# Eleven constant full-array matmuls a chunk between the reordering matmuls of a decode-attention kernel

## The chip, the cores and the metric

One core of one Trainium2 chip. The metric is the device time of one execution, in microseconds (us); times quoted are medians of the fast runs, three to eleven per kernel. A ratio compares runs of two kernels in the same rounds, and is not quite the ratio of the medians that are quoted beside it. One profiled run of each kernel gives the views shown.

## The reference, cut to what matters

Two attention decode steps with one query position each, concatenated. A has 32 query heads on 8 key heads and a window of 2048 keys; B has 32 heads, batch 4 and 8192 keys each.

```python
def _B_ref(x, k_cache, v_cache, wq, wo):
    B, Sq, D = x.shape                      # 4, 1, 512
    H, Dh = 32, 128
    q = (x @ wq).reshape(B, Sq, H, Dh) ...  # transposed to (B, H, Sq, Dh)
    scores = jnp.einsum("bhqd,bhkd->bhqk", q, k_cache) * (Dh ** -0.5)
    p = _softmax(scores, axis=-1)
    o = jnp.einsum("bhqk,bhkd->bhqd", p, v_cache)
    return ... @ wo                         # heads joined
```

B's two caches are 537 MB in bf16 (2 x 4 x 32 x 8192 x 128 x 2 bytes), so loading them is most of what the kernel must do.

## The kernel before

B is 32 chunks of 4 heads and one batch entry. A chunk has 256 key tiles and 256 value tiles of 128 x 128. TensorE, VectorE (DVE), ScalarE (ACT) and GpSimd (POOL) are the engines. This is the order in which a chunk's work is given to them; each engine then runs its own list and waits on semaphores (shortened, with comments added):

```python
def whole_B(c):
    ...
    for g in range(ch["NG"]):               # 32 groups of 8 key tiles
        emit_T(ch["s"] + g)                 # TensorE: 8 transposes; DVE or ACT: copy to SBUF
        ...
        if g >= SLAG:
            emit_S(ch["s"] + g - SLAG)      # TensorE: 8 score matmuls
    ...
    stats_rowmax(c, 1)
    reorder(c, 0, 0)                        # TensorE: 4 matmuls, 32 rows x 512 columns each
    reorder(c, 1, 1)
    reorder(c, 2, 2)
    stats_gmax(c)                           # TensorE: transpose of the row maxima; DVE: maximum
    stats_bc(c)                             # TensorE: broadcast; DVE: scaled bias
    exp_B(c)                                # ACT: 8 exponentials
    for u in range(3):
        take_wol(c, u, u)                   # DVE: copy of a reordered block
    reorder(c, 3, 0)                        # waits for take_wol(c, 0)
    take_wol(c, 3, 0)
    sums_B(c)
    for g in range(ch["NG"]):
        emit_pv(c, g)                       # TensorE: 8 value matmuls into the bank "po"
    ...
    norm_out(c)
```

`reorder(c, u, bank)` brings the output weights of the chunk's four heads into the order that the last product needs; block `u` uses the array rows 32u to 32u+31. `emit_pv` waits for the first four exponentials and for the values. The next chunk's values are loaded when the product of this chunk is done; its keys when the transposes of this chunk are. In the views `tr` takes transposes and reordered weights, `sc` scores, `ms` the small statistics, `po` the value product and `fin` the last product; `kv` holds keys or values, `pbb` the exponentials.

## Time and profile before

| | before |
|---|---|
| time, three runs ahead of the prediction | 1376.5 us |
| span of the profiled run | 1373.0 us |
| TensorE busy, DMA queue busy | 90%, 99.5% |
| mean granted TensorE clock | 0.915 |
| moved by DMA | 587 MB, mean 428 GB/s |

The granted clock is the share of full speed that TensorE was given. The prediction quotes the lines on the bound. What it says of the clock is seen in windows of 1 us in the middle of the span (columns: stretch, its length, busy us of TensorE, weight loads, DVE, ACT and POOL, granted clock, DMA share, GB/s):

```profile
619.00:620.00 1.00, 0.72 (x4) 0.10 (x2) 1.00 (x3) 0.97 (x3) 0.00 (x0) 1.00 0.60 262
620.00:621.00 1.00, 0.00 (x0) 0.00 (x0) 0.45 (x1) 0.96 (x3) 0.00 (x0) 0.65 0.99 426
...
624.00:625.00 1.00, 1.00 (x23) 1.00 (x21) 0.00 (x0) 0.00 (x0) 0.00 (x0) 0.50 1.06 459
...
628.00:629.00 1.00, 1.00 (x40) 1.00 (x37) 0.00 (x0) 0.00 (x0) 0.00 (x0) 1.00 1.07 459
```

The clock is halved at the end of the statistics (1.00 to 0.50 in these windows), and the value product's first microseconds run with it: 23 matmuls are seen in a microsecond, against 40 after the clock is back.

The statistics of the last chunk, in the timeline of TensorE (start, length, engine, line, operation, and in brackets the idle time before it and what ended it):

```profile
1354.86 1.06 PE L421 MATMUL tr<-wos,back 32*128 32x512 bf16 x12
1355.91 0.27 PE L419 MATMUL ms<-identf,rm 128*4 128x128 f32 x1
1356.55 0.38 PE L421 MATMUL ms<-gm,ind 4*128 4x4 f32 x2 [0.37 <-DVE gm L570]
1357.79 1.88 PE L421 MATMUL tr<-wos,back 32*128 32x512 bf16 x4 [0.86 <-DVE kv L716]
1359.60 7.23 PE L421 MATMUL po<-pbb,kv 128*128 128x64 bf16 x168
```

R stands for the start of the first line from here on, as in the prediction: 1354.86 in this chunk. The clock fell at 1357.58, 2.7 us after R, in the gap of 0.86 us, the longest of this timeline; in the 3.42 us up to there TensorE was busy for 2.09 us.

The trace also gives the pace of a reordering matmul of 512 columns: on one row group they start 0.216 us apart with the full clock (618.92, 619.13 and 619.35 in the chunk in the middle) and 0.427 us apart with the half (1358.18, 1358.61 and 1359.04).

### The profile page before, as it was taken

What the parts mean: (1) busy time and instruction counts of PE and PEld (TensorE: products, weight loads), DVE (VectorE), ACT (ScalarE), POOL (GpSimd) and SP (SyncE); (2) the same over time, 40 slices, a digit from 0 to 9 for tenths busy, and PEclk for the clock granted to TensorE, in tenths of its full rate; (3) what the DMA queues carried; (4) which work ended last, traced back from release to release, by engine and by line L of the source; (5) the groups of instructions that cost most, each with busy time, mean ns of one, the idle gap of its engine ahead of it and who ended that gap; (6) DMA issues with size and microseconds to landing.
All of it is one profiled execution on the core that took longest, in us unless ns stands there. A gap on an engine that the chain in (4) does not pass through costs nothing.

```text
span 1373.0 us, 60822 instructions
## 1 busy us (share of the span) xinstructions
PE 1229.9 (90%) x27417; PEld 1134.6 (83%) x27417; DVE 744.4 (54%) x1335; ACT 513.3 (37%) x649; POOL 9.8 (1%) x29
## 2 busy tenths in 40 slices
PE   4897899999898889998889898998988899988998
PEld 4786788889888788898888888987888889887887
DVE  1775456655555556555555565554555555554555
ACT  1553244433333334433333344243333443333333
POOL 2000000000000000000000000000000000000000
PEclk9998899999999999999999999998999899999999
DMA  9999999999999999999999999999999999999997
GB/s 401 425 427 443 422 422 435 432 431 436 437 432 428 431 432 432 434 438 435 433 432 420 433 435 430 437 439 430 428 430 432 431 435 439 433 428 430 422 428 319
DMA packets 21084, 587.52 MB, mean 428 GB/s; under 512 B 2356, under 2 KB 2376, under 8 KB 4808
## 3 DMA queue, kind: packets, MB, share of 16 engines
q1 hardware_dynamic: 21032, 587.21, 99.5%
q8 instruction: 15, 0.25, 0.1%
q14 instruction: 5, 0.04, 0.0%
q10 hardware_dynamic: 32, 0.01, 0.0%
HBM read 587.21 MB, written 0.01 MB: 428 GB/s over the span
## 4 chain that ended last, share of the span: by engine, by line
DMA 52%; PE 43%; DVE 2%; ACT 1%; issue 1%; SPq 0%; POOLq 0%; ACTq 0%; DVEq 0%
DMA kv<-in_B_v_cache_dram 47%; PE po L421 22%; PE tr L419 12%; PE sc L421 6%; DMA kv<-in_B_k_cache_dram 2%; DMA kv<-in_B_wq_dram 2%; PE ms L421 1%; PE tr L421 1%; ACT pbb L601 1%; DMA kv<-in_A_k_cache_dram 1%; PE fin L421 1%; DVE sA L539 1%; DVE kt L486 1%; PE ms L419 0%; DVE gm L570 0%
## 5 line engine op out<-in xcount | busy, mean ns | idle before, releaser
L419 PE MATMUL tr<-identb,kv 128*128 128x128 bf16 x8704 | 663.8, 220 | 9.3 <-POOLq L72 4.2
L484 ACT ACTIVATE kt<-tr 128x1024 bf16<-128x1024 bf16 x352 | 359.3, 1023 | 718.3 <-PE tr L419 718.0
L486 DVE COPY kt<-tr 128x1024 bf16<-128x1024 bf16 x736 | 501.8, 691 | 217.2 <-PE tr L419 214.4
L419 PEld LDWEIGHTS tr<-identb,kv 128*128 128x128 bf16 x8704 | 506.7, 98 | 20.3 <-issue 9.9
L421 PE MATMUL sc<-qq,kt 128*128 128x64 bf16 x8192 | 397.7, 191 | 13.7 <-DVE kt L486 9.8
L421 PEld LDWEIGHTS po<-pbb,kv 128*128 128x128 bf16 x8192 | 305.7, 108 | 74.0 <-issue 43.5
L421 PE MATMUL po<-pbb,kv 128*128 128x64 bf16 x8192 | 309.3, 208 | 51.7 <-POOLq L72 44.8
L421 PEld LDWEIGHTS sc<-qq,kt 128*128 128x128 bf16 x8192 | 331.2, 98 | 17.2 <-DVE kt L486 13.1
L601 ACT ACTIVATE pbb<-sc,negb 32x128 bf16<-32x128 f32 x256 | 137.2, 536 | 121.4 <-DVE negb L584 118.2
L421 PE MATMUL tr<-wos,back 32*128 32x512 bf16 x512 | 81.3, 409 | 27.4 <-DVE kv L716 27.4
L668 DVE RECIPROCAL rinv<-ms 128x4 f32<-128x4 f32 (+1 forms) x40 | 7.8, 196 | 167.5 <-PE ms L421 167.5
L716 DVE CAST kv<-tr 128x512 bf16<-128x512 f32 x128 | 81.2, 684 | 13.1 <-PE tr L421 13.1
L606 DVE TENSOR_REDUCE rsb<-pbb 128x4 f32<-128x1024 bf16 x32 | 39.0, 1220 | 50.9 <-ACT pbb L601 50.9
L421 PEld LDWEIGHTS tr<-wos,back 32*128 32x128 bf16 x512 | 23.5, 97 | 49.7 <-DVE kv L716 30.1
L555 DVE TENSOR_REDUCE rh<-sc 128x4 f32<-128x512 f32 x64 | 43.9, 686 | 14.3 <-PE sc L421 14.3
L690 DVE TENSOR_TENSOR oz<-po,rz 128x16 bf16<-128x16 f32 x32 | 5.6, 175 | 67.3 <-PE po L421 67.3
L421 PE MATMUL sc<-qb,kt 128*128 128x64 bf16 (+3 forms) x512 | 26.1, 196 | 0.6 <-DVE gx L576 0.6
L421 PEld LDWEIGHTS ms<-gm,ind 4*128 4x128 f32 x64 | 9.4, 182 | 18.0 <-DVE gm L570 18.0
L421 PEld LDWEIGHTS sc<-qb,kt 128*128 128x128 bf16 x512 | 21.8, 101 | 1.9 <-DVE gx L576 1.1
L421 PE MATMUL ms<-gm,ind 4*128 4x4 f32 x64 | 12.2, 258 | 11.9 <-DVE gm L570 11.9
L421 PE MATMUL po<-pba,kv 128*128 128x64 bf16 x512 | 20.5, 199 | 2.6 <-ACT pba L623 1.4
L421 PEld LDWEIGHTS po<-pba,kv 128*128 128x128 bf16 x512 | 17.9, 102 | 5.1 <-ACT pba L623 4.2
(63 smaller groups left out, 209.8 us busy)
## 6 DMA issues: line engine op xcount, KB each, us to landing
kv<-in_B_k_cache_dram SPq DMA_DIRECT2D x60, 4096.0 KB, 27.1
kv<-in_A_k_cache_dram SPq DMA_DIRECT2D x8, 2048.0 KB, 13.6
kv<-in_A_v_cache_dram SPq DMA_DIRECT2D x8, 2048.0 KB, 15.2
kv<-in_B_k_cache_dram SPq DMA_DIRECT2D x7, 2048.0 KB, 28.4
kv<-in_B_v_cache_dram SPq DMA_DIRECT2D x3, 4096.0 KB, 21.6
kv<-in_B_v_cache_dram SPq DMA_DIRECT2D x3, 2048.0 KB, 26.1
kv<-in_B_v_cache_dram SPq DMA_DIRECT2D x5, 1024.0 KB, 28.3
kv<-in_A_wq_dram SPq DMA_DIRECT2D x1, 4096.0 KB, 12.4
```

The source lines that it names most:

```text
L419: sch.add("pe", lambda e: e.transpose(o, l, r), waits, key)
L421: sch.add("pe", lambda e: e.matmul(o, l, r, start=start, stop=stop), waits, key)
L484: sch.add("act", lambda e: e.activation(dst, src, ACTF.Copy), waits=waits, key=("ev", s))
L486: sch.add("dve", lambda e: e.tensor_copy(dst, src), waits=waits, key=("ev", s))
L539: emit = lambda e, src=src, b=b: e.scalar_tensor_tensor(out=t, in0=src, scalar=mk[:, b:b + 1], in1=t, op0=ALU.mult, op1=ALU.add)
L555: sch.add("dve", lambda e: e.tensor_reduce(out=rh[:, half, :], in_=src, axis=AX.X, op=ALU.max), waits=[("S", ch["s"] + (half + 1) * ch["NG ...
L601: sch.add("act", lambda e, src=src, dst=dst, pp=pp, u=u: e.activation(dst, src, ACTF.Exp, bias=negb[pp, 0, u:u + 1], scale=scale), waits=[ ...
L606: sch.add("dve", lambda e: e.tensor_reduce(out=rst[1][:, :], in_=probs_of(c).rearrange("p j u -> p u j"), axis=AX.X, op=ALU.add), waits=[( ...
L668: sch.add("dve", lambda e: e.reciprocal(out=ri, in_=ms[:, L0:L0 + n]), waits=[("L", c)], key=("rinv", c))
L690: sch.add("dve", lambda e: e.tensor_tensor(out=o, in0=i0, in1=i1, op=ALU.mult), waits=waits, key=("oT", c))
L716: sch.add("dve", lambda e: e.tensor_copy(wol[:, u, :], o), waits=[("reord", c) if u == 3 else ("reord", c, u)] + [("fin", prev(c))], key=( ...
```

## The change

Its intent is to keep TensorE's array in use while the statistics wait for other engines, so that the clock is not halved. The eleven added matmuls, the fillers, multiply two constants and write the bank `po`, which nobody reads at that time; their result is overwritten by the value product.

```diff
+        def keep_busy(n):
+            for _ in range(n):
+                pe_mm(po[:, :], identb[:, :], sel4[:, :, :].rearrange("p r x -> p (r x)"))
+
         def whole_B(c):
...
             reorder(c, 2, 2)
+            keep_busy(2)
             stats_gmax(c)
+            keep_busy(1)
             stats_bc(c)
             exp_B(c)
             for u in range(3):
                 take_wol(c, u, u)
+            keep_busy(3)
             reorder(c, 3, 0)
+            keep_busy(5)
             take_wol(c, 3, 0)
```

## The prediction

> **What bounds the kernel now.** I read the page's summary first, then busy time and DMA rate by stretch, then the chain of waits, then the timeline of one chunk and of the last one.

> The program is decode attention: 8 chunks of A (135 us), then 32 chunks of B. In a B chunk TensorE transposes and scores 256 key tiles, does a short statistics part (maximum, exponentials, the reordering of the output weights), then multiplies 256 value tiles with the probabilities. The diff touches only that middle part.

> ```profile
> PE 1229.9 (90%) x27417; PEld 1134.6 (83%) x27417; DVE 744.4 (54%) x1335; ACT 513.3 (37%) x649; POOL 9.8 (1%) x29
> ...
> q1 hardware_dynamic: 21032, 587.21, 99.5%
> ...
> DMA 52%; PE 43%; DVE 2%; ACT 1%; issue 1%; SPq 0%; POOLq 0%; ACTq 0%; DVEq 0%
> ```

> Both TensorE (90%) and the DMA queue (99.5%) look full. Which one sets the end is told by the rate in each stretch (columns: stretch, its length, busy us of each engine, granted clock, DMA share, GB/s).

> ```profile
> 516.00:1219.00 703.00, 637.74 (x14347) 590.88 (x14345) 382.24 (x648) 261.34 (x324) 0.00 (x0) 0.91 1.00 433
> 1258.00:1295.30 37.30, 34.66 (x798) 32.45 (x799) 21.24 (x36) 14.54 (x18) 0.00 (x0) 0.95 1.00 425
> 1295.30:1332.10 36.80, 34.69 (x801) 32.49 (x801) 21.18 (x36) 14.53 (x18) 0.00 (x0) 0.95 1.01 427
> 1360.00:1365.00 5.00, 5.00 (x107) 5.00 (x105) 1.62 (x2) 1.54 (x3) 0.00 (x0) 0.56 0.87 349
> 1365.00:1373.00 8.00, 5.22 (x161) 4.80 (x157) 0.96 (x4) 0.00 (x0) 0.00 (x0) 1.00 0.02 8
> ```

> The reader is to see that the DMA share is 1.00 at 425 to 433 GB/s until about 1365 us, whoever the chain names, and that only the last 8 us have no transfer. Bytes over rate: one B chunk is 2 x 8.39 MB, at 433 GB/s 38.7 us. TensorE's own period where it waits for no data (the two stretches from 1258.5) is 36.8 us. So in the long middle TensorE waits some 2 us a chunk for values to land, and time saved there only lengthens the wait. The next lines are one such chunk: the statistics, and the wait for values before the first value matmul.

> ```profile
> 615.76 1.06 PE L421 MATMUL tr<-wos,back 32*128 32x512 bf16 x12
> 616.81 0.27 PE L419 MATMUL ms<-identf,rm 128*4 128x128 f32 x1
> 617.45 0.38 PE L421 MATMUL ms<-gm,ind 4*128 4x4 f32 x2 [0.37 <-DVE gm L570]
> 618.69 1.03 PE L421 MATMUL tr<-wos,back 32*128 32x512 bf16 x4 [0.85 <-DVE kv L716]
> 623.23 6.81 PE L421 MATMUL po<-pbb,kv 128*128 128x64 bf16 x168 [3.50 <-POOLq L72]
> 632.86 28.96 DMA kv<-in_B_v_cache_dram
> ```

> The next values are issued when the product of this chunk ends (632.86) and land 28.96 us later. Of that, 8.39 MB at 433 GB/s is 19.4 us; the other 9.6 us the transfer queues behind keys issued before. Issuing it earlier lets it queue longer, not land earlier.

> **The clock.** In this chunk the granted clock falls to half at 620.35 us and returns at 627.1. I located every fall and return in the B chunks in windows of 0.25 us: all lie on one grid of 3.413 us. Cold, value matmuls come every 53 ns (64 columns at half clock: 1 us holds about 19); warm, 88 take 2.71 us, 30.8 ns each. In the last chunk:

> ```profile
> 1357.79 1.88 PE tr L421 x4
> 1359.67 7.17 PE po L421 x168
> 1367.03 2.60 PE po L421 x88
> 1369.98 0.62 PE fin L421 x8
> ```

> The fall is at 1357.58 and the return at 1364.41, so four reordering matmuls take 1.88 us (1.03 us warm) and 4.74 us of the value product run cold: 89 matmuls that would take 2.73 us warm, a loss of 2.0 us. This is what the change is after.

> [...] 0.50 and 1.00 are the levels, and the grid is 3.413 us. The trace adds that the window need not be idle: the fall at 1357.58 closes a window in which TensorE was busy for some 2.1 of 3.41 us. [...]

> **The change part by part.** Nothing is removed, no DMA or wait is added, and the instruction orders of VectorE, ScalarE and the DMA queue are unchanged. TensorE gets 11 matmuls of 512 columns a chunk, which write a bank nobody reads then: 2 before the maximum's transpose, 1 before its broadcast, 3 before and 5 after the last reordering. [...]

> With R the start of the 12 reordering matmuls, in a chunk that waits for no data: the 12 end issuing about R+0.85, two fillers reach R+1.28, and the transpose, at R+1.05 before, starts 0.25 us late. The one filler fits in the 0.37 us gap before the broadcast, the three in the 0.86 us gap before the last reordering. All the rest shifts by 0.25 us: last reordering at R+3.2, 0.85 us warm, five fillers 1.08 us, so the value product starts at R+5.1. Before, it started at R+4.54 to 4.74 in the last three chunks (bounded by the exponentials or by the cold reordering). Cost: 0.4 to 0.55 us a chunk. Gain, if the clock holds: the product takes 256 x 30.8 ns = 7.9 us plus 0.1.

> Does the clock hold? I weighted each matmul by the share of the array's rows that it uses. Before, the window from R-1.36 to R+2.05 (48% so weighted) was not followed by a fall, that from R-1.05 to R+2.36 (40%) was. A fall thus needs somewhat under half. After the change the worst window (R+0.85 to R+4.26) has 0.43+0.21+0.64+0.21+0.21 = 1.70 of 3.41 us, 50%, without the transpose. It is close, but above. I give 65% that the clock holds where TensorE waits for no data. Where it waits for values, idle time follows the fillers and the clock may fall as before; there it costs nothing.

> **The sum.** The last keys before TensorE leads land at 1258.3 in any case. From there: in the 30th and the 31st B chunk the product ran cold for one window, 3.4 us, a loss of 1.4 us (64 tiles at 53 instead of 30.8 ns), less 0.5 = 0.9 us each; the last saves 2.0 - 0.4 = 1.6. That is 3.4 us. But the last value pieces set a floor:

> ```profile
> kv<-in_B_v_cache_dram SPq DMA_DIRECT2D x2, 256.0 KB, 31.6
> ```

> They are issued up to 1334.4 and land about 1366.0, because the queue is full; earlier issue does not help. The last eight tiles then take 0.25 us: product ends at 1366.25 at the earliest, instead of 1369.6. So the gain is capped at 3.3 us: 1376.5 - 3.3 = 1373.2 us if all holds.

> **The rivals.**
> 1. *The whole cold loss comes back:* 32 chunks x 2.0 us = 64 us, 4.6% faster. For it speak TensorE's 90% and the 43% of the chain. Against it: the DMA share of 1.00 and the 9.6 us of queueing[...]. I give this 1%.
> 2. *The clock falls anyway, and the fillers run cold.* From R+3.2 the last chunk's work is 0.85+1.08+7.9 us warm, with half of the 6.35 us up to the return added: product ends at R+16.1 instead of R+14.7, 1.4 us later; over three chunks up to 4 us, 1380 us. The 50% against a threshold between 40 and 48% speaks against it, the rough weighting for it. 15%.
> 3. *It holds in some of the three chunks* (the grid's phase decides), fillers and gains cancel: 1375 to 1376.5 us. 20%.
> 4. *Fillers delay the middle:* 38.3 us of TensorE work even with cold fillers (36.8+1.5) stays below 38.7 us, and 9.6 us of queue hide a late issue. No effect.

> **Range and chances.** 0.65 x 1373.2 + 0.2 x 1375.7 + 0.15 x 1379 is 1374.6; the most likely outcome is near 1373.5. I say 1374.0, with 1372.0 to 1377.8 for 8 in 10 (the three runs before spread by 1 us). A 2% step is 27.5 us, which only the first rival reaches, or a DMA effect that I don't see.

> **What would show it.** Right: DMA share 1.00 and 433 GB/s in the middle as before; TensorE's wait for values longer by about what it saves; last transfer again near 1365 us; granted clock 1.00 through the last three chunks; product of the last chunk ending about 1366 to 1367. Wrong, if the clock falls within R+2.4 to R+5.8 in the last chunks (step "the clock holds"), if the value product starts much later than R+5.1[...], or if the period of the middle moves off 38.8 us (the DMA bound).

## The result, and the profile after

| | before | after |
|---|---|---|
| time, six runs each | 1376.74 us (1375.67 to 1378.51) | 1373.45 us (1372.49 to 1374.21) |
| ratio | | 0.9975, 95% interval 0.9962 to 0.9988 |
| span of the profiled run | 1373.0 us | 1371.8 us |
| mean granted clock | 0.915 | 0.981 |

The page of the changed kernel, the same three lines as in the prediction:

```profile
PE 1249.8 (91%) x27769; PEld 1110.4 (81%) x27769; DVE 744.0 (54%) x1335; ACT 513.8 (37%) x649; POOL 9.8 (1%) x29
...
q1 hardware_dynamic: 21032, 587.21, 99.6%
...
DMA 57%; PE 39%; DVE 2%; issue 1%; ACT 0%; SPq 0%; POOLq 0%; DVEq 0%
```

and its stretches:

```profile
516.00:1219.00 703.00, 650.00 (x14544) 578.06 (x14544) 382.38 (x648) 261.62 (x324) 0.00 (x0) 0.99 1.00 432
...
1355.00:1360.00 5.00, 4.74 (x36) 1.93 (x37) 3.42 (x8) 2.06 (x4) 0.00 (x0) 1.00 0.98 416
1360.00:1365.00 5.00, 5.00 (x156) 4.65 (x155) 1.51 (x2) 2.27 (x5) 0.00 (x0) 1.00 0.93 375
1365.00:1371.80 6.80, 4.03 (x120) 3.61 (x116) 0.95 (x4) 0.00 (x0) 0.00 (x0) 1.00 0.06 21
```

The clock of the middle went from 0.91 to 0.99 and the bytes per second stayed (433, 432). TensorE's records are busier by 12 us of 703 although the product is faster, because the fillers count as busy. The saving shows only in the last stretches, where the clock is 1.00 and the transfers come to their end.

The last chunk's statistics in the changed kernel:

```profile
1355.21 1.06 PE L421 MATMUL tr<-wos,back 32*128 32x512 bf16 x12
...
1356.20 0.61 PE L421 MATMUL po<-sel,identb 128*128 128x512 bf16 x2
...
1356.65 0.27 PE L419 MATMUL ms<-identf,rm 128*4 128x128 f32 x1
...
1357.29 0.38 PE L421 MATMUL ms<-gm,ind 4*128 4x4 f32 x2 [0.16 <-DVE gm L570]
...
1357.60 0.82 PE L421 MATMUL po<-sel,identb 128*128 128x512 bf16 x3
...
1358.53 1.03 PE L421 MATMUL tr<-wos,back 32*128 32x512 bf16 x4
...
1359.49 1.25 PE L421 MATMUL po<-sel,identb 128*128 128x512 bf16 x5
...
1360.58 5.06 PE L421 MATMUL po<-pbb,kv 128*128 128x64 bf16 x168
```

The reader is to see a price and a gain. The price: the transpose starts at R+1.44 instead of R+1.05, and the product at R+5.37 instead of R+4.74. The gain: 168 value tiles take 5.06 us instead of 7.23, and the reordering of four 1.03 instead of 1.88. From R to the end of the span it was 18.14 us (1373.0 - 1354.86) and is 16.59 us (1371.8 - 1355.21), 1.55 us less.

Where did the middle's time go? The waits of TensorE name it. "POOLq L72" is the relay by which POOL passes on that a transfer has landed; the figures are us in total, times, and the longest. Before:

```profile
PE po L421 <- POOLq L72: 44.8, 23, 3.5
...
PE tr L419 <- POOLq L72: 4.2, 8, 0.7
```

After:

```profile
PE tr L419 <- POOLq L72: 42.3, 26, 1.9
PE po L421 <- POOLq L72: 22.6, 23, 2.0
```

Before, the product waited for values. Now fillers occupy part of that wait, the product ends sooner, and the transposes of the next chunk wait for keys instead: 4.2 us became 42.3. Both waits are for the same queue of transfers, which is full (busy for 99.5% of the span before and 99.6% after).

Even near the end keys gate TensorE once. The chain of waits of the changed kernel, from there to the end (start, us, what; the x173 are five fillers and 168 value tiles):

```profile
1306.73 31.11 DMA kv<-in_B_k_cache_dram
1337.94 0.62 PE tr L419 x8
...
1359.56 6.09 PE po L421 x173
1365.84 2.60 PE po L421 x88
1368.79 0.62 PE fin L421 x8
```

One caution about the pair of profiles: in the run profiled after, values land 1.2 us later throughout (the product of the chunk in the middle starts at 624.39 instead of 623.23), though nothing in the diff changes a transfer, and the profiled run before was a fast one (1374.7 us by its own clock). So the spans differ by 1.2 us and the medians by 3.3. Lengths counted from R don't have this offset.

### The profile page after: what moved, and what is told of

The parts are those of the page before. It is cut to its first block, busy times and chain, and to the rows that moved or that the text cites. A ratio compares the mean times of both kernels' runs of the same rounds, so it can differ in the third digit from the quotient of the medians.

```text
span 1371.8 us, 61526 instructions
## 1 busy us (share of the span) xinstructions
PE 1249.8 (91%) x27769; PEld 1110.4 (81%) x27769; DVE 744.0 (54%) x1335; ACT 513.8 (37%) x649; POOL 9.8 (1%) x29
## 3 DMA queue, kind: packets, MB, share of 16 engines
q1 hardware_dynamic: 21032, 587.21, 99.6%
HBM read 587.21 MB, written 0.01 MB: 428 GB/s over the span
## 4 chain that ended last, share of the span: by engine, by line
DMA 57%; PE 39%; DVE 2%; issue 1%; ACT 0%; SPq 0%; POOLq 0%; DVEq 0%
DMA kv<-in_B_k_cache_dram 36%; DMA kv<-in_B_v_cache_dram 18%; PE tr L419 18%; PE po L421 9%; PE sc L421 8%; DMA kv<-in_B_wq_dram 2%; PE fin L421 1%; PE ms L421 1%; PE tr L421 1%; DMA kv<-in_A_k_cache_dram 1%; DVE sA L539 1%; DVE kt L486 0%; DVE kv L716 0%; ACT pba L623 0%; DVE rm L551 0%
## 5 line engine op out<-in xcount | busy, mean ns | idle before, releaser
L419 PE MATMUL tr<-identb,kv 128*128 128x128 bf16 x8704 | 668.6, 221 | 48.2 <-POOLq L72 42.3
L419 PEld LDWEIGHTS tr<-identb,kv 128*128 128x128 bf16 x8704 | 510.3, 99 | 61.1 <-DVE qq L495 41.2
L421 PE MATMUL sc<-qq,kt 128*128 128x64 bf16 x8192 | 399.3, 192 | 13.5 <-DVE kt L486 9.8
L421 PEld LDWEIGHTS sc<-qq,kt 128*128 128x128 bf16 x8192 | 332.9, 98 | 16.9 <-DVE kt L486 13.1
L421 PEld LDWEIGHTS po<-pbb,kv 128*128 128x128 bf16 x8192 | 250.9, 99 | 37.1 <-issue 20.5
L421 PE MATMUL po<-pbb,kv 128*128 128x64 bf16 x8192 | 253.8, 194 | 24.1 <-POOLq L72 22.6
L421 PE MATMUL po<-sel,identb 128*128 128x512 bf16 x352 | 96.9, 384 | 0.0
L716 DVE CAST kv<-tr 128x512 bf16<-128x512 f32 x128 | 80.0, 683 | 0.0
L421 PE MATMUL tr<-wos,back 32*128 32x512 bf16 x512 | 67.8, 383 | 3.2
L421 PEld LDWEIGHTS po<-sel,identb 128*128 128x128 bf16 x352 | 26.6, 98 | 47.6 <-issue 27.8
L421 PEld LDWEIGHTS tr<-wos,back 32*128 32x128 bf16 x512 | 21.5, 93 | 34.0 <-DVE kv L716 18.9
L570 DVE TENSOR_REDUCE gm<-ms 4x4 f32<-4x128 f32 x40 | 11.2, 279 | 28.6 <-PE ms L419 28.6
L421 PE MATMUL sc<-qb,kt 128*128 128x64 bf16 (+3 forms) x512 | 26.3, 197 | 0.4 <-DVE gx L576 0.4
L421 PEld LDWEIGHTS ms<-gm,ind 4*128 4x128 f32 x64 | 9.4, 182 | 17.5 <-DVE gm L570 17.5
L421 PEld LDWEIGHTS sc<-qb,kt 128*128 128x128 bf16 x512 | 22.1, 102 | 1.6 <-issue 0.9
```

What stands on the lines that cost most here:

```text
L419: sch.add("pe", lambda e: e.transpose(o, l, r), waits, key)
L421: sch.add("pe", lambda e: e.matmul(o, l, r, start=start, stop=stop), waits, key)
L570: sch.add("dve", lambda e: e.tensor_reduce(out=gm[0:C, m, 0:U], in_=src, axis=AX.X, op=ALU.max), waits=[("trm", c)], key=("gmax", c))
L716: sch.add("dve", lambda e: e.tensor_copy(wol[:, u, :], o), waits=[("reord", c) if u == 3 else ("reord", c, u)] + [("fin", prev(c))], key=( ...
```

## The experiments

All runs were timed in five rounds. Two theories on where the 3.3 us come from: *tail*, by which the middle is bound by transfers and only TensorE's time in the last three chunks reaches the end; and *middle*, by which each of the 32 chunks gives about 0.1 us. Two on the means: the fillers act by the *activity of the array*, or any instruction on TensorE would do.

### Half of the value product left out

```diff
-            for t in range(TG):
+            for t in (range(TG) if c < NCA else (0, 2, 5, 7)):   # in emit_pv
```

> The changed kernel with half of the value matmuls of B left out (tiles 0, 2, 5 and 7 of each eight; the result is wrong on purpose, all bytes are still loaded): TensorE works about 3.9 us less in every B chunk, 125 us in all. Theory 'transfers bound the middle': only the tail shrinks; last value piece lands about 1366 to 1367 us as before, the end comes at most 2 us sooner, 1371 to 1373 us, ratio 0.996 to 0.9975, 431 to 433 GB/s in the middle. Rival 'TensorE sets part of the middle': 1330 us or lower, over 2% faster.

Measured: 1371.71 us (before in the same rounds 1377.23), ratio 0.9962 (0.9949 to 0.9975); the result is wrong, as meant. Its middle, its wait for keys, and the end of its chain:

```profile
516.00:1219.00 703.00, 609.47 (x12223) 533.76 (x12239) 383.72 (x648) 262.01 (x324) 0.00 (x0) 0.94 1.00 432
```

```profile
PE tr L419 <- POOLq L72: 123.0, 30, 5.6
```

```profile
1330.02 36.23 DMA kv<-in_B_v_cache_dram
1366.99 0.62 PE fin L421 x8
```

TensorE was relieved of about 125 us against the changed kernel, and the time is 1.7 us under that kernel's (timed in other rounds) and 5.5 us under the kernel before: 432 GB/s again, the relief became a wait for keys of 123 us, and the last value piece sets the end. With the fetching order as it is, 1371.7 us is about the floor for a faster product; the change took 3.3 us of the some 5 there were. The theory *TensorE sets part of the middle* falls.

### Fillers in some of the chunks only

Chunks that differ can't share one loop, so TensorE's loop of B chunks is split in two ahead of the last three.

```diff
-            keep_busy(5)          # and the 2, 1 and 3 likewise
+            keep_busy(5 if c >= NC - 3 else 0)      # "last three"
+            keep_busy(5 if c < NC - 3 else 0)       # "first 29"
```

> Fillers only in the last three of the 32 B chunks; the loop of the chunks is split in two for it. Theory 'tail' (the middle is bound by transfers, only the last three chunks' TensorE time reaches the end): the whole gain stays, 3 us under the kernel before, ratio 0.9975 +- 0.001; granted clock half in part of the first 29 chunks, 1.00 in the last three. Rival 'middle' (each chunk gives about 0.1 us): 3/32 of the gain, 0.3 us, ratio 0.9998. Mixed: ratio about 0.9985.

> Fillers in the first 29 B chunks only, the complement of the run before, with the same split loop. Theory 'tail': no gain, ratio 1.000 +- 0.001, clock near 1.00 in the middle and half for one or two grid windows in each of the last three chunks. Rival 'middle': 29/32 of the gain, ratio 0.9978.

Measured: last three 1380.49 us, ratio 1.0028 (1.0016 to 1.0040); first 29 1382.78 us, ratio 1.0046 (1.0033 to 1.0059). Both missed: they are slower than the kernel before. So I ran the two controls, the kernels with no fillers and with all, split in the same way (an empty segment between the chunks, seen by TensorE alone):

> Control for the two runs with the split loop: the kernel before, without fillers, with its TensorE loop split before the last three B chunks in the same way. Both those runs were slower than the kernel before by 3.3 and 5.5 us, and their traces show TensorE stalled 8 to 10 us in the first chunk after the split. If the split costs that and fillers in the first 29 chunks are worth nothing (theory 'tail'), this run equals the run with fillers in the first 29 only: 1382.5 +- 1 us. Rival 'middle': 3 us more than that, 1385.5 us.

> The changed kernel (fillers in all 32 chunks) with the same split loop. Theory 'tail': equals the run with fillers in the last three only, 1380.5 +- 1 us, and is about 2 us under the split kernel without fillers. Rival 'middle': 2 to 3 us under the run with fillers in the last three, 1377.5 us.

| split kernels | fillers | time | ratio to before | R of the third last chunk |
|---|---|---|---|---|
| none | 0 | 1382.27 us | 1.0041 (1.0027 to 1.0054) | 1286.50 |
| first 29 | 0 to 28 | 1382.78 us | 1.0046 (1.0033 to 1.0059) | 1289.65 |
| last three | 29 to 31 | 1380.49 us | 1.0028 (1.0016 to 1.0040) | 1286.37 |
| all | 0 to 31 | 1378.52 us | 1.0016 (1.0002 to 1.0030) | 1286.51 |

The split itself costs 5.5 us. In the timeline of the kernel with no fillers, the chunk after the split has gaps for which the timeline shows no cause but issue:

```profile
1264.71 0.56 PE L419 MATMUL tr<-identb,kv 128*128 128x128 bf16 x7 [0.42 <-issue]
1271.13 0.26 PE L421 MATMUL sc<-qq,kt 128*128 128x64 bf16 x3 [0.95 <-issue]
1278.18 0.39 PE L421 MATMUL sc<-qq,kt 128*128 128x64 bf16 x8 [1.62 <-issue]
1285.04 0.38 PE L419 MATMUL tr<-identb,kv 128*128 128x128 bf16 x4 [1.49 <-issue]
```

The DMA records say more: queue q8, of the kind `instruction` on the page, has 22 transfers here and 15 in the kernel before. Seven of 16 KB come after the split, and four of them start some 2.5 us before the ends of these four gaps (1262.13, 1268.71, 1275.83, 1282.52). The gaps are 4.5 us in all, and that TensorE waited in them for its instructions is my estimate from these times; no run varied it.

With the split common to all four, fillers in the first 29 chunks alone give nothing (1382.27 and 1382.78). The third last chunk's statistics begin at the same time with and without fillers ahead of it (1286.51 and 1286.50; in the profiled run of "first 29", 1.7 us slower than its median, 3 us later): 29 chunks of fillers did not bring TensorE there any sooner. That is *tail*, and *middle* falls.

The control with all fillers was not as expected: I had said it would equal "last three", and it is 2 us under it. The two profiled runs show a difference that is not in the middle either. The third last chunk, with its stalls, had a half clock for 10.2 us in "last three" (from R+0.7 to R+10.95), and for 3.4 us in "all" (R+0.0 to R+3.4); from R to the end of its product it took 19.26 and 16.22 us. That this holds for the medians too is likely, but one trace of each doesn't show it. Why the clock came back one window after the fall in one of them and three windows in the other was not tried further.

### Fillers over a quarter of the rows

```diff
-    pe_mm(po[:, :], identb[:, :], sel4[:, :, :].rearrange("p r x -> p (r x)"))
+    pe_mm(po[:, :], identb[0:32, :], sel4[0:32, :, :].rearrange("p r x -> p (r x)"))
```

> The same eleven fillers of 512 columns at the same places, but over 32 rows of the array in place of 128 (same time while warm, a quarter of the active array). Theory 'array activity holds the clock': the clock falls again in the last three chunks, fillers cost their time cold: the value product starts at R+6 to R+7 and ends 1 to 1.5 us later a chunk than in the kernel before; 1377 to 1381 us, ratio 1.001 to 1.003; the mean clock is back near 0.91. Rival 'any instruction on TensorE holds the clock': as the changed kernel, ratio 0.9975, clock 0.98.

Measured: 1377.94 us, ratio 1.0003 (0.9990 to 1.0016); the middle and the last chunk's statistics:

```profile
516.00:1219.00 703.00, 671.25 (x14545) 603.73 (x14542) 382.17 (x648) 261.68 (x324) 0.00 (x0) 0.91 1.00 432
```

```profile
1363.30 0.39 PE L421 MATMUL tr<-wos,back 32*128 32x512 bf16 x1 [0.19 <-DVE kv L716]
1363.31 0.39 PE L421 MATMUL po<-sel,identb 32*128 32x512 bf16 x1
...
1364.92 1.30 PE L421 MATMUL po<-pbb,kv 128*128 128x64 bf16 x28 [0.36 <-ACT pbb L601]
```

The clock is back at 0.91, and the gain is gone, with as many instructions as in the changed kernel and TensorE busy for 671 of 703 us. So the activity of the array counts, not TensorE's busy time; the rival *any instruction* falls. (Whether it is the rows or the quarter of the data that counts, this run can't tell.) The price I expected did not come: the fillers use rows 0 to 31 and the last reordering rows 96 to 127, and the two run side by side (starts 1363.30 and 1363.31), so the product starts at R+4.89 (R+5.75 in the chunk before) and not at R+6 to R+7.

### More and fewer fillers

```diff
             reorder(c, 3, 0)
-            keep_busy(5)
+            keep_busy(10)      # or 2, or 0
```

> The changed kernel with ten instead of five fillers after the last reordering: the suspected cost doubled. [...] the value product starts at R+6.45 where no transfer gates it, instead of R+5.37. Theory 'only the last chunk's TensorE time reaches the end': middle unchanged at 38.8 us a chunk, the end 1.1 us later (up to 2.2 if the chunk before the last is not hidden by keys still on their way), 1374.5 to 1375.7 us. Rival 'each chunk pays': 32 x 1.08 = 35 us, 1408 us.

> The changed kernel with two instead of five fillers after the last reordering. The value product may start 0.65 us earlier after R, at R+4.7. If a window needs somewhat under half of the array's time (my reading of the falls in the kernel before), three fillers fewer leave 1.06 to 1.3 of 3.41 us in the worst window, 31 to 38%, and the clock falls in most chunks, so the product runs cold again for 3.4 to 6.8 us: time as before or 1 us better, 1375.5 to 1377 us, mean clock 0.91 to 0.94. Rival 'five are more than needed': the clock holds (0.98), and the time is 0.5 us under the changed kernel.

> The changed kernel with no filler after the last reordering (2, 1, 3, 0). Product at R+4.9 (0.39 us of delay by the two at the head, then bound by the exponentials). Re-reading the traces of five runs, windows in which the array's rows were in use under 0.37 of the time were followed by a fall and those over 0.38 (nearly all) were not. Here the worst window has 0.31 to 0.37: the clock falls in the chunks whose grid meets it, some of the 32, and mean clock is 0.93 to 0.97; the end depends on the last chunk's phase: 1372.5 to 1375.5 us. Rival 'fillers at the tail are needed': clock 0.91 to 0.92 and 1376 us.

and without the two at the head, with the five kept:

```diff
             reorder(c, 2, 2)
-            keep_busy(2)
             stats_gmax(c)
```

> The changed kernel without the two fillers ahead of the maximum's transpose (0, 1, 3, 5). The transpose is at R+1.05 again, all later steps 0.39 us earlier, product at R+4.97. Worst window 0.42 to 0.48, over 0.38: the clock holds (0.97 to 0.98). Time 0.4 us under the changed kernel, 1372.5 to 1373.3 us; the difference is too small for the ratio, the trace decides by the start of the product after R.

| fillers (head, gap, before and after the last reordering) | time | ratio | clock | product starts in the last chunk |
|---|---|---|---|---|
| 2, 1, 3, 10 | 1376.96 us | 1.0016 (1.0002 to 1.0030) | 0.991 | R+6.45 |
| 2, 1, 3, 5 (the change) | 1373.45 us | 0.9975 (0.9962 to 0.9988) | 0.981 | R+5.37 |
| 2, 1, 3, 2 | 1372.84 us | 0.9976 (0.9962 to 0.9990) | 0.968 | R+4.93 |
| 2, 1, 3, 0 | 1373.52 us | 0.9985 (0.9971 to 0.9999) | 0.950 | R+4.93 |
| 0, 1, 3, 5 | 1372.99 us | 0.9980 (0.9967 to 0.9994) | 0.978 | R+4.98 |

Ten fillers delay the product by the 1.08 us expected, and cost more than expected: 3.5 us by the medians instead of at most 2.2. In that trace R follows R by 37.07 us in both of the last steps, where the changed kernel has 36.00 and, with its wait for keys, 36.62. With 1.07 us more from the last R to the product's end, that is 2.6 us: each of the last three chunks pays, and keys hide part of it once. The rest of the 3.5 us is not seen in this trace, whose run was the fastest of its five (1375.10). The middle hid them (432 GB/s); the rival of 35 us falls.

With two fillers after the last reordering my expectation was wrong: the clock held in the last three chunks, where I had it fall in most. With none it fell in 23 of the 32 chunks, but in only one of the last three, and the time went up a little. With two at most the exponentials set the product's start, not the fillers (R+4.93; with none TensorE waited 0.59 us for them in the last chunk). The other two came as expected. Among these four without the ten the times are too close for their intervals to part; only the starts are told apart, by the trace.

### Fillers that delay nothing

The last reordering goes into `po` with the other three, on its own rows, and is copied out first; the fillers fill only the wait for the exponentials. Until `po` is free again, they add zeros onto unused rows of the output bank, over half of the array's columns.

```diff
             reorder(c, 2, 2)
-            keep_busy(2)
+            reorder(c, 3, None)           # None: into po
             stats_gmax(c)
-            keep_busy(1)
+            keep_half(1)                  # zeros x constants, added to fin[64:128]
             stats_bc(c)
+            keep_half(3)
             exp_B(c)
+            take_wol(c, 3, None)
             for u in range(3):
                 take_wol(c, u, u)
-            keep_busy(3)
-            reorder(c, 3, 0)
-            keep_busy(5)
-            take_wol(c, 3, 0)
+            keep_busy(7, [("wol", c, 3)])
```

(The first of the seven fillers waits for `take_wol(c, 3)`, and the product comes after them on TensorE. The zero tile and the new bank in `reorder` and `take_wol` are left out here.)

> Fillers that delay nothing: the fourth reordering goes into the bank of the value product together with the other three, is read first, and fillers fill only the wait for the exponentials: one and three of half height (64 columns of the array, zeros added onto unused rows), then seven full ones once the bank is free again. Product expected at R+4.55 instead of R+5.37, clock held (worst window about 53%): the last chunk's product ends 0.8 us earlier after R than in the changed kernel; if no transfer gates it, 1372.0 to 1373 us; floor by the halved value product 1371.7 us. If half-height fillers count less than half: clock falls in part of the chunks, 1374 to 1376 us.

Measured: 1371.76 us against 1376.78 of before, ratio 0.9967 (0.9954 to 0.9981), result correct, clock 0.984. Its last chunk, whose R is 1353.99:

```profile
1355.04 0.27 PE L421 MATMUL ms<-identf,rm 128*4 128x128 f32 x1
...
1356.00 0.83 PE L423 MATMUL fin<-sel,zw 128*64 128x512 bf16 x3
1357.15 1.46 PE L423 MATMUL po<-sel,identb 128*128 128x512 bf16 x6 [0.32 <-DVE kv L718]
1358.54 5.07 PE L423 MATMUL po<-pbb,kv 128*128 128x64 bf16 x168
```

The transpose is at R+1.05 as before the change, the product at R+4.55, and it runs warm. By its median this is the fastest correct kernel, level with the floor of the halved product (1371.71 us), and its ratio to before leaves out 1; it is 1.7 us under the changed kernel by the medians, but their intervals overlap.

## Why the prediction was right, point by point

- *The middle is bound by transfers.* Right: 433 and 432 GB/s, and half of the value product left out gives no more than 5.5 us.
- *The change saves at the end only.* Right, shown by the split kernels. The cap of 3.3 us was reached by the medians (3.29), but not by my sum, so that the medians meet it is in part luck: in the profiled pair the last chunk gave 1.55 us (1.6 expected), and the two before it 0.84 us (1.8 expected), from 96.34 us (1258.52 to 1354.86) to 95.50 us (1259.71 to 1355.21). TensorE alone saves 0.68 us a chunk there (R to R 36.73 and 36.05), because the product starts later than I said, and keys took back the rest in the last chunk. That is 2.4 us in all, inside the interval of the ratio; 0.9 us of the 3.29 is seen in no trace.
- *The value product starts at R+5.1.* Off: R+5.37. The two fillers at the head delay the transpose by 0.39 us, not 0.25, and the four last reordering matmuls hold TensorE for 0.96 us (1358.53 to 1359.49) and not 0.85. The fillers themselves were right: five take 1.09 us (1359.49 to 1360.58).
- *The clock holds in the last chunks, at 65%.* It held, but the share behind the number, below which I expected a fall, was mis-sized. I put it at between 40% and 48%, from a weighting by eye; the estimate over all windows gives those two windows 0.31 and 0.40, and sorts best near 0.37. So the step that I held for the weakest had room, which the runs with fewer fillers show. That it would fall where TensorE waits for values was mostly wrong too: the mean clock of the middle is 0.99.
- *TensorE waits longer for values.* Wrong in its object: the wait for values halved and a wait for keys of 42 us came up. The place of the slack moved along the chain; its worth, nothing, stayed.
- *The last transfer near 1365 us, the product's end at 1366 to 1367.* The product ended at 1368.4 us; 1.2 us of that is the profiled run's later transfers. The last pieces of values were no floor here: the last lands at 1367.2, 1.2 us before the product's end. They gate the halved product, not the changed kernel.

The rivals: the whole cold loss coming back (64 us) and the fillers running cold did not happen. (The second rival's sum gives R+16.2, not R+16.1.) The third, fillers and gains that cancel, is what the kernel with ten fillers is.

## What to carry to other kernels

A clock that is halved for 3.4 to 10.2 us in each of 32 chunks looks like 64 us to win; ask first what TensorE waits for next. TensorE had slack here (it waited for transfers anyway), and the some 125 us less of the halved product became a wait for keys of 123 us; only the stretch that no transfer hides counted, the last three chunks. Where fillers are worth it, place them in waits that are there anyway (the product then started at R+4.55, with the change at R+5.37), and see to it that they use many rows of the array: over 128 rows the clock of the middle was 0.99, over 32 rows 0.91. More of them than needed cost their time in the chunks that no transfer hides: five more put the product 1.08 us later after R. When chunks are made to differ for an experiment, run the split alone as a control, for here it cost 5.5 us, more than the 3.3 us under study.
